# An attention and two mixture stages on one core: the first stage re-ordered, and one group's H spilled in two parts

## The chip, the cores and the metric

One core of a Trainium2 chip runs the whole program. The time is device microseconds of one execution, the median over several runs. TensorE (PE) multiplies matrices into PSUM; VectorE (DVE) and ScalarE (ACT) read PSUM; GpSimd (POOL) works on SBUF; SyncE (SP) issues most of the loads. Each engine takes its instructions in a fixed order.

## The reference, cut to what matters

Three stages follow each other; `x` of a stage is the output of the one before.

```python
    scale = 1.0 / np.sqrt(D)
    scores = scale * np.matmul(q, k.transpose(0, 1, 3, 2))
...
    keep = is_sink | in_window
    scores = np.where(keep, scores, -1000000000.0)
    scores = scores - np.max(scores, axis=-1, keepdims=True)
    a = np.exp(scores)
    a = a / (np.sum(a, axis=-1, keepdims=True) + 1e-09)
    return np.matmul(a, v).astype(np.float32)
...
    h = np.maximum(np.maximum(x @ w1, x @ w2), x @ w3)
    return (h @ w_out).astype(np.float32)
...
    for e in range(E):
        mask = assigned == e
        h = np.maximum(x[mask] @ w1[e], 0.0)
        out[mask] = h @ w2[e]
```

q, k and v are 4 x 8 x 768 x 64 (batch, heads, positions, head size), the window is 128, the sinks are 4. The rows of the attention are 3072 x 512; d_ff is 768 in the second stage; the third has 8 experts of at most 384 tokens, and each token goes to one.

## The kernel before, in words

Attention runs in 32 units. A unit is one batch, one half of 384 positions and one pair of heads: `load`, `prep`, `score`, `soft`, `pv`. Four units (p = 0 to 3) make a group g, which is a block of 384 tokens by 512; the 8 groups are called a0 to a7 in the order strings. The units of a0 and a1 are "native": their products are made in plain fp32, with no split of q and k (`native=8`). The later units split each operand into a rounded high part and the rest (h and l), and multiply three of the four products.

Moe1 takes a group's four x tiles, splits each into `xh`, `xl` (L265 to L269), and makes for each of six slices f three sums of 12 products (L280), whose maximum `m` (L282, L283) is one slice of H. H is split into h and l as well, and `x2` (L294) multiplies it with the out weights, 18 products for each of six sums (L305). The 18 weight slices come as words of 8 bytes, and `single` and `split` turn each into fp32 and then into h and l: one load (L220), DVE (L225, L227), ACT (L226, L212) and POOL (L228, L213). The first four loads land in a ring that later becomes the tile HL. The six out-weight slices (`load_out`) go through two buffers `st` of the pool conv, and start with transposes and small products that use a PSUM tile of the scores.

HL is not free while the ring is in use. So group 0 writes its six `m` slices to DRAM (L285), group 1 keeps its H in HL, and after group 1's x2 the six slices of group 0 are loaded (`reload`, L317), split by ACT (L323) and DVE (L324) into HL, and multiplied.

The order of the work is written as two strings, of units and of weight slices (`w` is one f of the three matrices, `o` one out-weight slice), and a planner inside the block (`schedule_with_timeline_sim`) lays the instructions out engine by engine from its own timeline. Some instructions are emitted with priority. SP's and ACT's transfers stand in the same orders as all else that the engine issues, so a transfer that has to wait for its buffer holds what stands behind it.

In `score` (L110) a block of scores that isn't the first of its half is copied from PSUM by ACT (L134), and then DVE writes the masked block over it (L135). T, the tile of probabilities, has three buffers for all units.

Of the kernel before, what the change touches and what calls it, by code (L numbers as in the profile page):

```python
# [22 lines left out]
def f32(ap): return ap.bitcast(FT)  # L23
def flip(nc,out,x,ident):
    nc.tensor.transpose(out,x,f32(ident))  # L25

class Attn:
    def __init__(s, tc, q,k,v,vs, keep, consts, pst, psp, pss, psv, work):
        s.tc=tc; s.nc=nc=tc.nc; s.q,s.k,s.v,s.vs=q,k,v,vs
        s.pst,s.psp,s.pss,s.psv,s.w=pst,psp,pss,psv,work  # L30
        jp=work.tile([128,128],I32,name="jp",tag="qs0",bufs=2)
        nc.gpsimd.iota(jp,pattern=[[1,128]],base=0,channel_multiplier=-1)
        s.ident=keep.tile([128,128],FR,name="ident")
        nc.vector.tensor_scalar(s.ident,jp,0.0,None,op0=OP.is_equal)
# [12 lines left out]
        s.kf=[]; s.kz=[s.zeros([consts.tile([128,4,132],FR,name=f"kz{h}") for h in range(2)])]  # L47
        t=consts.tile([1,1],FT,name="one"); nc.vector.memset(t,0.0)
        nc.scalar.activation(t,t,AF.Exp)
        s.n=0; s.no=('kh0','kh1')  # L50
        s.extra=None
# [8 lines left out]
    def load(s,b,hf,p,native=False):  # L60
        nc=s.nc; w=s.w
# [11 lines left out]
        else:  # L73
            u['kn']=w.tile([128,4,132],FT,name="kn",bufs=1)
            nc.sync.dma_start(u['kn'][:,:nb],s.k[i,:,:nb*132].rearrange("p (c j) -> p c j",j=132))
            u['qn']=w.tile([128,384],FT,name="qn",bufs=1)
            nc.sync.dma_start(u['qn'],s.q[i])
            u['vn']=w.tile([128,4,2,64],FT,name="vn",bufs=1)
# [31 lines left out]
    def score(s,u):  # L110
# [4 lines left out]
        for i in range(3):  # L115
# [4 lines left out]
            for h in range(2):  # L120
# [11 lines left out]
                else:  # L132

                    nc.scalar.activation(t[:,132*h:132*h+132],ps[:,128*h:128*h+132],AF.Copy)  # L134
                    nc.vector.copy_predicated(block,s.ca[:,h,:],ps[:,132-132*h:260-132*h])  # L135
# [12 lines left out]
    def pv(s,u,x):  # L148
# [9 lines left out]
        for h in range(2):  # L158
# [8 lines left out]
            if nat:  # L167
# [3 lines left out]
                for c,n,q,blk in jobs:  # L171
                    nc.tensor.matmul(po[a,q:q+n],u['vn'][:,blk,h,:],Af[:,c:c+n],start=False,stop=True,skip_group_check=True)  # L172
                if h==1: nc.scalar.activation(x,po[:,:384],AF.Copy)
                continue
# [7 lines left out]
            nc.tensor.matmul(po[:,:384],u['VK'][:,h,:],PB,start=False,stop=True,skip_group_check=True)  # L182
            nc.scalar.activation(x[a,:],po[o,:384],AF.Copy)
            nc.vector.tensor_tensor(x[a,:],po[a,:384],x[a,:],op=OP.add)

# [17 lines left out]
class Moe1:  # L203
    def __init__(s, tc, words,wgate, consts, wpool, main, conv, mm, pt, pss, ident):
        s.tc=tc; s.nc=tc.nc; s.mm=mm; s.pss=pss; s.main=main; s.conv=conv; s.ident=ident; s.consts=consts
        s.src=words; s.wgate=wgate
        s.W=[[wpool.tile([128,4,768],FR,name=f"w{i}{x}") for x in "hl"] for i in range(3)]
        s.WO=None; s.at=None; s.stage=None; s.HL=None; s.n=0
        s.WG=main.tile([128,6,16],FR,name="wgt")
# [4 lines left out]
    def single(s,src,ring=False):  # L214
# [4 lines left out]
        else: st=s.conv.tile([128,512,2],I32,name="st",bufs=2)  # L219
        nc.sync.dma_start(st.rearrange("p n t -> p (n t)"),src.bitcast(I32))  # L220
        A=s.pss.tile([128,512],FT,name="ps").bitcast(I32); C=st[:,:,0]
# [6 lines left out]
        nc.gpsimd.tensor_tensor(R,R,C,op=OP.add)  # L228
        return R.bitcast(FT)
    def part(s,x,f):  # L230
        return s.HL[:,"hl".index(x)*6+f]
# [28 lines left out]
    def group(s,xs,spill=None,pool=None,mid=None,between=None):  # L260
# [3 lines left out]
        for p in range(4):  # L264
            h=main.tile([128,384],FR,name=f"xh{p}",bufs=1); l=main.tile([128,384],FR,name=f"xl{p}",bufs=1)  # L265
            with s.tc.high_priority():
                nc.scalar.activation(h,xs[p],AF.Copy)  # L267
                nc.vector.tensor_tensor(l,xs[p],f32(h),op=OP.subtract)  # L268
            X.append((h,l))  # L269
        H=[]  # L270
        if s.HL is None and spill is None: s.HL=main.tile([128,12,384],FR,name="HL")
        for f in range(6):
            if between is not None: between(f)
            m=main.tile([128,384],FT,name="hm",bufs=2)
            for i in range(3):
# [8 lines left out]
                if mid is not None and (f,i)==s.at: mid()  # L284
            if s.HL is None: nc.scalar.dma_start(spill[f],m); continue  # L285
            h,l=(pool.tile([128,384],FR,name=f"h{x}{f}",bufs=1) if pool else s.part(x,f) for x in "hl")
            with s.tc.high_priority():
# [29 lines left out]
    def reload(s,spill):  # L317
        nc=s.nc; H=[]
# [304 lines left out]

def attention_mixtures(tc,q,k,v,vs,words,wg,u1,u2,out,off=60,spread=(0,1,3,4),native=8,order='a0 a0 a0 a0 w a1 w a1 w w a1 w w a1 a2',order1='a2 o o o o o o a2 a2',back=1,at=(1,0),s1=300,s2=400,nring=6):
    nc=tc.nc
    PS=bass.MemoryType.PSUM
    with ExitStack() as ctx:
# [12 lines left out]
        def att(g,p):  # L640
            xs.setdefault(g,[])
            u=A.load(g//2,g%2,p,4*g+p<native); A.prep(u); A.score(u); A.soft(u)
            x=main.tile([128,384],FT,name=f"x{p}")
            A.pv(u,x); xs[g].append(x)
        def lw(f): M.load_w(f)
        def lo(f): M.load_out(f)
        with tc.block(schedule_with_timeline_sim=True):
            A.extra=Spare(main)
            A.kf=[A.zeros([A.extra.tile([128,4,132],FT,tag=f'kf{i}{h}') for h in range(2)]) for i in range(3)]
            def emit(o,p):  # L650
                n=cnt[o]=cnt.get(o,-1)+1
# [11 lines left out]
            for o in order.split(): emit(o,False)  # L663
            rest=None
            for g in range(NG):
# [7 lines left out]
                d = g>=NG-3  # L673
                if g==0: sp=[dram.tile([128,384],FT,name=f"sp{f}") for f in range(6)]
                if g==NG-3: sp2=[[dram.tile([128,384],FT,name=f"sp{f}{x}") for x in "hl"] for f in range(6)]
                if g==NG-1:
# [3 lines left out]
                    r=Route(tc,LG,rt,rw,rc)  # L680
                H6,H=H if g==NG-1 else None,M.group(xs[g],sp if g==0 else sp2 if g==NG-3 else None,hp if g==NG-1 else None,rest,between)
                while late: between(spread[0])
# [39 lines left out]
        M.x2(H6,T7-3,LG,x2d,256,hp)  # L722
        M.by_rows(sp2,T7-6,x2d,acc,hp)
        with tc.high_priority(): fet(0)
# [64 lines left out]
```

## Time and profile before

| what | value |
|---|---|
| median of 3 runs | 983.9 us (982.41 to 985.26) |
| the profiled execution | 985.81 us, of which 984.0 us are the span from the first to the last instruction |
| PE busy | 937.8 us (95%), 6552 products |
| DVE, ACT, POOL busy | 687.8, 533.8, 348.8 us |
| mean granted TensorE clock | 0.977 of full speed |

PE is busy for nearly the whole span, so what counts is where it isn't, and where its clock is granted at half. Times below are from the start of the span. The prediction takes them from four kinds of views: busy time in stretches, waits by engine, groups of instructions by line, and instructions in order of time.

### The profile page before, as it was taken

The page shows a single profiled execution, that of the slowest core. Times are in us where ns is not written, and L with a number is a line of the kernel's source. Part 1 is how long each engine was busy: PE and PEld are TensorE (multiplying, and loading weights), DVE is VectorE, ACT ScalarE, POOL GpSimd, SP SyncE. Part 2 cuts the span into 40 slices and gives each one's busy share as a digit, 9 for nine tenths or more (in the row PEclk, how much of TensorE's full clock was granted, in tenths as well). Part 3 has the DMA queues.
Part 4 walks back from the last instruction along what each step waited for, and adds up shares of the span by engine and source line. Part 5 has one row for each costly group of instructions (what it writes and reads, how often), then busy time and mean ns, then how long its engine had stood idle before and what let it go on. Part 6 is the DMA issues. An engine that isn't in the chain of part 4 may idle for free.

```text
span 984.0 us, 18469 instructions
## 1 busy us (share of the span) xinstructions
PE 937.8 (95%) x6552; PEld 857.8 (87%) x6552; DVE 687.8 (70%) x1807; ACT 533.8 (54%) x1425; POOL 348.8 (35%) x317
## 2 busy tenths in 40 slices
PE   5889999969999999999999999999999999999996
PEld 4568989959999999999999998888888888888895
DVE  3897676687879976776764344879989889873320
ACT  4666664788789777677663211233433434344431
POOL 3578357145555535425434000011113032043331
PEclk8899999989999999999999999999999999999999
DMA  7455121222112112112110002544345352454420
GB/s 226 151 170 172 50 77 64 68 83 88 53 40 78 52 49 73 28 48 81 64 50 12 1 1 76 164 154 130 119 149 174 98 172 99 160 189 154 135 81 32
DMA packets 50541, 95.03 MB, mean 97 GB/s; under 512 B 6704, under 2 KB 20784, under 8 KB 50448
## 3 DMA queue, kind: packets, MB, share of 16 engines
q1 hardware_dynamic: 40560, 71.57, 23.4%
q0 software_dynamic: 3840, 12.45, 3.6%
q10 hardware_dynamic: 6048, 9.83, 2.7%
q8 instruction: 51, 0.84, 0.4%
q14 instruction: 42, 0.34, 0.1%
HBM read 77.84 MB, written 16.12 MB: 95 GB/s over the span
## 4 chain that ended last, share of the span: by engine, by line
PE 75%; DVE 8%; ACT 6%; issue 5%; DMA 4%; POOL 1%; SPq 1%; POOLq 0%; ACTq 0%; DVEq 0%
PE mm L280 28%; PE mm L608 11%; PE acc L601 11%; PE mm L305 7%; PE po L181 3%; PE rc L406 2%; PE pt L25 2%; PE pp L25 2%; PE po L172 2%; PE ps L126 1%; PE ps L127 1%; DMA sa<-in_u_dram 1%; PE ps L123 1%; DVE A_w L163 1%; DVE qs L97 1%
## 5 line engine op out<-in xcount | busy, mean ns | idle before, releaser
L601 PE MATMUL acc<-wbh,HL 128*128 128x512 f32 x384 | 131.1, 398 | 0.0
L177 POOL TENSOR_TENSOR L<-A_w,H 128x768 fp32r<-128x768 f32 x46 | 87.0, 1891 | 101.5 <-ACT H L176 91.1
L283 DVE TENSOR_TENSOR hm<-mm,hm 128x384 f32<-128x384 f32 x96 | 53.3, 555 | 68.6 <-PE mm L280 65.1
L620 POOL DMA_INDIRECT out_dram<-og,idx x24 | 32.2, 1340 | 180.6 <-ACT og L619 177.3
L305 PE MATMUL mm<-woh,HL 128*128 128x260 f32 (+1 forms) x432 | 89.5, 296 | 2.0 <-DVE HL L324 1.1
L552 ACT ACTIVATE wah<-sa 128x512 fp32r<-128x512 f32 x64 | 40.5, 632 | 89.6 <-PE mm L608 72.2
L601 PEld LDWEIGHTS acc<-wbh,HL 128*128 128x128 f32 x384 | 71.5, 188 | 12.8
L552 ACT ACTIVATE wbh<-sb 128x512 fp32r<-128x512 f32 x64 | 40.4, 631 | 74.9 <-PE acc L601 72.0
L601 PE MATMUL acc<-wbl,HL 128*128 128x512 f32 x192 | 76.9, 401 | 0.0
L305 PEld LDWEIGHTS mm<-woh,HL 128*128 128x128 f32 x432 | 72.3, 198 | 3.3 <-DVE HL L324 1.4
L608 PE MATMUL mm<-HL,wah 128*128 128x384 f32 x256 | 68.5, 343 | 0.0
L280 PE MATMUL mm<-xh,w0h 128*128 128x384 f32 x192 | 66.8, 348 | 1.2 <-ACT xh L267 0.6
L280 PE MATMUL mm<-xh,w1h 128*128 128x384 f32 x192 | 66.7, 347 | 0.8 <-ACT hm L282 0.5
L280 PE MATMUL mm<-xl,w0h 128*128 128x384 f32 x192 | 65.5, 341 | 1.9 <-DVE xl L268 1.9
L280 PE MATMUL mm<-xh,w2h 128*128 128x384 f32 x192 | 67.0, 349 | 0.0
L280 PE MATMUL mm<-xh,w1l 128*128 128x384 f32 x192 | 65.5, 341 | 0.0
L280 PE MATMUL mm<-xl,w2h 128*128 128x384 f32 x192 | 65.5, 341 | 0.0
L553 DVE TENSOR_TENSOR wbl<-sb,wbh 128x512 fp32r<-128x512 f32 x64 | 43.9, 688 | 30.7 <-ACT wbh L552 30.7
L280 PE MATMUL mm<-xl,w1h 128*128 128x384 f32 x192 | 65.1, 339 | 0.0
L280 PE MATMUL mm<-xh,w0l 128*128 128x384 f32 x192 | 65.1, 339 | 0.0
L280 PE MATMUL mm<-xh,w2l 128*128 128x384 f32 x192 | 65.1, 339 | 0.0
L612 DVE SCALAR_TENSOR_TENSOR HL<-mm,HL 128x384 fp32r<-128x384 f32 x64 | 35.5, 554 | 40.8 <-ACT HL L611 40.6
(320 smaller groups left out, 2888.3 us busy)
## 6 DMA issues: line engine op xcount, KB each, us to landing
sa<-in_u_dram SPq DMA_DIRECT2D x64, 256.0 KB
sb<-in_u_dram SPq DMA_DIRECT2D x64, 256.0 KB
HL<-in_words_dram SPq DMA_DIRECT2D x18, 512.0 KB
qn<-in_q_dram SPq DMA_DIRECT2D x24, 192.0 KB
x2d<-xo ACTq DMA_DIRECT2D x15, 256.0 KB
kn<-in_k_dram SPq DMA_DIRECT2D x12, 264.0 KB
st<-in_words_dram SPq DMA_DIRECT2D x6, 512.0 KB
vn<-in_v_dram SPq DMA_DIRECT2D x12, 256.0 KB
```

The costliest lines, as they stand in the source:

```text
L25: nc.tensor.transpose(out,x,f32(ident))
L177: nc.gpsimd.tensor_tensor(L,Af,f32(H),op=OP.subtract)
L181: nc.tensor.matmul(po[:,q:q+n],u['VS'][:,blk,128*h:128*h+128],part[:,c:c+n],start=(part is H and j==0),stop=False,skip_group_check=True)
L280: nc.tensor.matmul(ps[:,:384],s.W[i][a][:,p,f*128:(f+1)*128],X[p][b],start=(n==0),stop=(n==11)); n+=1
L283: else: nc.vector.tensor_tensor(m,ps[:,:384],m,op=OP.max)
L305: nc.tensor.matmul(ps[:,:n],H[f][a][:,t*128:(t+1)*128],s.WO[b][:,f,u,c],start=(k==0),stop=(k==17)); k+=1
L552: nc.scalar.activation(h,src,AF.Copy)
L553: (nc.gpsimd if s.n>=6 and nm=="wa" else nc.vector).tensor_tensor(l,src,f32(h),op=OP.subtract)
L601: s.mms.append(nc.tensor.matmul(acc[t],H[f][a][:,t*128:(t+1)*128],W[f][1][b],start=(f==0 and n==0),stop=(f==F-1 and n==2))); n+=1
L608: s.mms.append(nc.tensor.matmul(ps[:,:384],W[f][0][a][:,k,:],X[k][b],start=(n==0),stop=(n==11))); n+=1
L612: nc.vector.scalar_tensor_tensor(l,ps[:,:384],0.0,f32(h),op0=OP.max,op1=OP.subtract)
L620: st=nc.gpsimd.indirect_dma_start(out=s.out,out_offset=bass.IndirectOffsetOnAxis(ap=idx[:,t:t+1],axis=0),in_=o,in_offset=None)
```

## The change

Six edits, all in the attention and moe1 block.

1. The score copies of the first four units go from ACT to DVE.
2. The units of a1 move ahead by one or two places among the weight slices.
3. `pv` of a0's units writes the pair `xh`, `xl` straight from PSUM (`split`: ACT copies, DVE subtracts), so `group` has nothing left to split there.
4. Two orders of loads are given to the planner: the first a2 unit's k and q loads come after the last word load of the ring, and an out-weight load after the sixth word load from the end. The two memsets of `kz` come after the six of `kf`.
5. Group 0's H is split at once into `hp` tiles, which take the `st` buffers of conv, and both parts are written to DRAM: 12 transfers of 192 KB in place of 6.
6. `reload` only loads, 12 transfers: f 0 to 3 into the `xh`, `xl` tiles, f 4 and 5 into HL. ACT and DVE have nothing to do there.

```diff
+def split(nc,hl,x):
+    nc.scalar.activation(hl[0],x,AF.Copy)
+    nc.vector.tensor_tensor(hl[1],x,f32(hl[0]),op=OP.subtract)
...
-            nc.sync.dma_start(u['kn'][:,:nb],s.k[i,:,:nb*132].rearrange("p (c j) -> p c j",j=132))
+            ld=[nc.sync.dma_start(u['kn'][:,:nb],s.k[i,:,:nb*132].rearrange("p (c j) -> p c j",j=132))]
-            nc.sync.dma_start(u['qn'],s.q[i])
+            ld.append(nc.sync.dma_start(u['qn'],s.q[i]))
+            if s.behind is not None:
+                for x in ld: s.tc.add_manual_dep(x.ins,s.behind.ins.name,mybir.DependencyInfo(mybir.DependencyClass.NoSync,mybir.DependencyReason.DATA),reason="order of loads")
+                s.behind=None
...
-                    nc.scalar.activation(t[:,132*h:132*h+132],ps[:,128*h:128*h+132],AF.Copy)
+                    if u['n']<4: nc.vector.tensor_copy(t[:,132*h:132*h+132],ps[:,128*h:128*h+132])
+                    else: nc.scalar.activation(t[:,132*h:132*h+132],ps[:,128*h:128*h+132],AF.Copy)
...
-                if h==1: nc.scalar.activation(x,po[:,:384],AF.Copy)
+                if h==1:
+                    for c in x: split(nc,c,po[:,:384]) if type(c) is tuple else nc.scalar.activation(c,po[:,:384],AF.Copy)
...
-        nc.sync.dma_start(st.rearrange("p n t -> p (n t)"),src.bitcast(I32))
+        ld=nc.sync.dma_start(st.rearrange("p n t -> p (n t)"),src.bitcast(I32))
+        if ring: s.loads.append(ld)
+        else: s.tc.add_manual_dep(ld.ins,s.loads[-6].ins.name,mybir.DependencyInfo(mybir.DependencyClass.NoSync,mybir.DependencyReason.DATA),reason="order of loads")
...
-            if s.HL is None: nc.scalar.dma_start(spill[f],m); continue
-            h,l=(pool.tile([128,384],FR,name=f"h{x}{f}",bufs=1) if pool else s.part(x,f) for x in "hl")
+            if s.HL is None: h,l=(s.conv.tile([128,2,384],FR,name="hp",tag="st",bufs=2)[:,x] for x in range(2))
+            else: h,l=(pool.tile([128,384],FR,name=f"h{x}{f}",bufs=1) if pool else s.part(x,f) for x in "hl")
...
-            m=s.main.tile([128,384],FT,name="hm",bufs=2)
-            nc.sync.dma_start(m,spill[f])
-            h,l=s.part("h",f),s.part("l",f)
-            nc.scalar.activation(h,m,AF.Copy)
-            nc.vector.tensor_tensor(l,m,f32(h),op=OP.subtract)
-            H.append((h,l))
+            H.append([s.main.tile([128,384],FR,name=f"x{x}{f}",bufs=1) if f<4 else s.part(x,f) for x in "hl"])
+            for d,x in zip(spill[f],H[f]): s.nc.sync.dma_start(f32(x),d)
...
+            A.zeros(A.kz[0])
...
+                if o=='a2': A.behind=M.loads[-1]
...
+                if g in (0,NG-3): sp=[[dram.tile([128,384],FT,name=f"sp{g}{f}{x}") for x in "hl"] for f in range(6)]
...
-order='a0 a0 a0 a0 w a1 w a1 w w a1 w w a1 a2'
+order='a0 a0 a0 a0 w a1 w a1 w a1 w a1 w w a2'
```

## Rows read from the trace of the kernel before

**Rows 1.** Busy time in stretches, whole span; after the bounds PE, PEld, DVE, ACT, POOL.
```profile
0.00:36.00 36.00, 23.83 (x77) 16.12 (x77) 19.27 (x60) 20.85 (x75) 13.97 (x27) 0.76 0.64 194
36.00:68.00 32.00, 26.33 (x124) 18.15 (x125) 28.09 (x50) 21.08 (x74) 23.15 (x23) 0.95 0.57 182
68.00:124.00 56.00, 56.00 (x324) 50.06 (x323) 41.81 (x84) 35.08 (x108) 36.35 (x36) 1.00 0.34 112
124.00:181.00 57.00, 55.26 (x357) 53.17 (x356) 37.94 (x78) 32.83 (x78) 32.06 (x29) 1.00 0.21 66
181.00:237.00 56.00, 47.77 (x339) 45.16 (x339) 45.40 (x86) 50.18 (x156) 21.39 (x16) 0.88 0.28 86
237.00:320.00 83.00, 81.74 (x568) 80.69 (x568) 68.35 (x132) 70.21 (x206) 44.61 (x40) 1.00 0.19 58
```

**Rows 2.** What PE waited for, 0 to 36 us; total, times, longest.
```profile
PE ps L123 <- POOL woh L53: 4.8, 1, 4.8
PE ps L123 <- DVE T_w L135: 1.7, 1, 1.7
PE ps L123 <- DVE wol L135: 1.3, 1, 1.3
PE ps L123 <- DMA qf<-in_q_dram: 0.5, 1, 0.5
```

**Rows 3.** Groups of ACT, 0 to 36 us; the idle time before them stands last.
```profile
L134 ACT ACTIVATE T_w<-ps 128x132 f32<-128x132 f32 x12 | 3.1, 270 | 6.9 <-PE ps L123 6.8
L226 ACT ACTIVATE HL<-HL 128x512 int32<-128x512 uint32 x4 | 2.6, 660 | 5.0 <-DMA HL<-in_words_dram 5.0
L94 ACT ACTIVATE kh_w<-kn 64x396 fp32r<-64x396 f32 x4 | 2.1, 529 | 0.1
```

**Rows 4.** Groups of DVE, 0 to 36 us.
```profile
L135 DVE COPY_PREDICATED T_w<-ca,ps 128x128 f32<-128x128 uint8 x10 | 2.9, 301 | 4.4 <-ACT T_w L134 4.3
```

**Rows 5.** SP's transfers in order of time: start, time taken to issue.
```profile
14.93 0.35 SPq L71 DMA_DIRECT2D qf<-in_q_dram  x1
15.85 0.58 SPq L75 DMA_DIRECT2D kn<-in_k_dram  x1
64.08 12.31 SPq L220 DMA_DIRECT2D HL<-in_words_dram  x5
```

**Rows 6.** Short stretches: PE's busy time and, third from the end, its clock.
```profile
12.00:16.00 4.00, 1.60 (x7) 0.97 (x7) 0.99 (x5) 3.02 (x15) 0.00 (x0) 1.00 0.95 284
20.00:32.00 12.00, 8.64 (x26) 5.65 (x28) 7.53 (x20) 11.22 (x44) 1.84 (x3) 0.50 0.65 189
208.00:212.00 4.00, 3.30 (x16) 3.30 (x17) 4.00 (x7) 3.11 (x15) 2.35 (x2) 0.53 0.33 90
220.00:224.00 4.00, 2.87 (x13) 2.87 (x14) 3.84 (x8) 3.21 (x11) 3.48 (x3) 0.50 0.40 104
```

**Rows 7.** What PE waited for, 36 to 68 us.
```profile
PE mm L280 <- DVE xl L268: 1.9, 3, 1.1
PE mm L280 <- ACT xh L267: 0.6, 1, 0.6
```

**Rows 8.** POOL and ACT in order of time: the last weight slice, the sixth slice's eviction.
```profile
102.31 1.28 POOL L213 TENSOR_TENSOR w2l<-HL,w2h 128x512 fp32r<-128x512 f32 x1
117.24 0.49 ACT L282 ACTIVATE hm<-mm 128x384 f32<-128x384 f32 x1
```

**Rows 9.** Groups of ACT, 181 to 237 us.
```profile
L323 ACT ACTIVATE HL<-hm 128x384 fp32r<-128x384 f32 x6 | 3.1, 516 | 2.1 <-DMA hm<-sp 2.1
L94 ACT ACTIVATE kh_w<-kn 64x528 fp32r<-64x528 f32 x8 | 5.1, 641 | 0.1
```

**Rows 10.** What PE waited for, 181 to 237 us.
```profile
PE ps L126 <- DVE T_w L135: 4.3, 3, 2.0
PE mm L305 <- DVE HL L324: 1.1, 1, 1.1
```

**Rows 11.** A group of the page's costliest, whole span.
```profile
L283 DVE TENSOR_TENSOR hm<-mm,hm 128x384 f32<-128x384 f32 x96 | 53.3, 555 | 68.6 <-PE mm L280 65.1
```

More of the change, by code (lines that the diff above doesn't have):

```diff
@@ L46, in __init__ @@
             t=consts.tile([128,384],FR,name=f"psb{i}"); nc.vector.memset(f32(t),0.0); s.pb.append(t)
-        s.kf=[]; s.kz=[s.zeros([consts.tile([128,4,132],FR,name=f"kz{h}") for h in range(2)])]
+        s.kf=[]; s.kz=[[consts.tile([128,4,132],FR,name=f"kz{h}") for h in range(2)]]
         t=consts.tile([1,1],FT,name="one"); nc.vector.memset(t,0.0)
         nc.scalar.activation(t,t,AF.Exp)
-        s.n=0; s.no=('kh0','kh1')
+        s.behind=None; s.n=0; s.no=('kh0','kh1')
         s.extra=None
@@ L182, in pv @@
             nc.tensor.matmul(po[:,:384],u['VK'][:,h,:],PB,start=False,stop=True,skip_group_check=True)
-            nc.scalar.activation(x[a,:],po[o,:384],AF.Copy)
-            nc.vector.tensor_tensor(x[a,:],po[a,:384],x[a,:],op=OP.add)
+            nc.scalar.activation(x[0][a,:],po[o,:384],AF.Copy)
+            nc.vector.tensor_tensor(x[0][a,:],po[a,:384],x[0][a,:],op=OP.add)
 class Spare:
@@ L207, in __init__ @@
         s.W=[[wpool.tile([128,4,768],FR,name=f"w{i}{x}") for x in "hl"] for i in range(3)]
-        s.WO=None; s.at=None; s.stage=None; s.HL=None; s.n=0
+        s.WO=None; s.at=None; s.stage=None; s.HL=None; s.n=0; s.loads=[]
         s.WG=main.tile([128,6,16],FR,name="wgt")
@@ L229, in single, with pair @@
         return R.bitcast(FT)
+    def pair(s,p):
+        return tuple(s.main.tile([128,384],FR,name=f"x{x}{p}",bufs=1) for x in "hl")
     def part(s,x,f):
@@ L264, in group @@
         for p in range(4):
[L265 to L269, printed above, removed]
+            if type(xs[p]) is tuple: X.append(xs[p]); continue
+            X.append(s.pair(p))
+            with s.tc.high_priority(): split(nc,X[p],xs[p])
         H=[]
@@ L317, in reload @@
     def reload(s,spill):
-        nc=s.nc; H=[]
+        H=[]
         for f in range(6):
-            m=s.main.tile([128,384],FT,name="hm",bufs=2)
-            nc.sync.dma_start(m,spill[f])
-            h,l=s.part("h",f),s.part("l",f)
-            nc.scalar.activation(h,m,AF.Copy)
-            nc.vector.tensor_tensor(l,m,f32(h),op=OP.subtract)
-            H.append((h,l))
+            H.append([s.main.tile([128,384],FR,name=f"x{x}{f}",bufs=1) if f<4 else s.part(x,f) for x in "hl"])
+            for d,x in zip(spill[f],H[f]): s.nc.sync.dma_start(f32(x),d)
         return H
@@ L622, in expert, with attention_mixtures @@
             s.scat.append(st)
-def attention_mixtures(tc,q,k,v,vs,words,wg,u1,u2,out,off=60,spread=(0,1,3,4),native=8,order='a0 a0 a0 a0 w a1 w a1 w w a1 w w a1 a2',order1='a2 o o o o o o a2 a2',back=1,at=(1,0),s1=300,s2=400,nring=6):
+def attention_mixtures(tc,q,k,v,vs,words,wg,u1,u2,out,off=60,spread=(0,1,3,4),native=8,order='a0 a0 a0 a0 w a1 w a1 w a1 w a1 w w a2',order1='a2 o o o o o o a2 a2',back=1,at=(1,0),s1=300,s2=400,nring=6):
     nc=tc.nc
@@ L642, in att @@
             u=A.load(g//2,g%2,p,4*g+p<native); A.prep(u); A.score(u); A.soft(u)
-            x=main.tile([128,384],FT,name=f"x{p}")
-            A.pv(u,x); xs[g].append(x)
+            x=main.tile([128,384],FT,name=f"x{p}") if g else M.pair(p)
+            A.pv(u,[x]); xs[g].append(x)
         def lw(f): M.load_w(f)
@@ L662, in emit @@
                         A.kz.append(A.zeros([A.extra.tile([128,4,132],FR,name=f'kz{h}b') for h in range(2)]))
-            for o in order.split(): emit(o,False)
+            for o in order.split():
+                if o=='a2': A.behind=M.loads[-1]
+                emit(o,False)
             rest=None
@@ L673, in attention_mixtures @@
                 d = g>=NG-3
-                if g==0: sp=[dram.tile([128,384],FT,name=f"sp{f}") for f in range(6)]
-                if g==NG-3: sp2=[[dram.tile([128,384],FT,name=f"sp{f}{x}") for x in "hl"] for f in range(6)]
+                if g in (0,NG-3): sp=[[dram.tile([128,384],FT,name=f"sp{g}{f}{x}") for x in "hl"] for f in range(6)]
                 if g==NG-1:
@@ L680, in attention_mixtures @@
                     r=Route(tc,LG,rt,rw,rc)
-                H6,H=H if g==NG-1 else None,M.group(xs[g],sp if g==0 else sp2 if g==NG-3 else None,hp if g==NG-1 else None,rest,between)
+                H6,H=H if g==NG-1 else None,M.group(xs[g],sp if g in (0,NG-3) else None,hp if g==NG-1 else None,rest,between)
                 while late: between(spread[0])
@@ L722, in attention_mixtures @@
         M.x2(H6,T7-3,LG,x2d,256,hp)
-        M.by_rows(sp2,T7-6,x2d,acc,hp)
+        M.by_rows(sp,T7-6,x2d,acc,hp)
         with tc.high_priority(): fet(0)
```

## The prediction

> **What bounds the kernel now.** I read the busy time by stretch first [rows 1]. PE is busy for 937.8 of 984.0 us, so the change can only win what PE doesn't use, and the stretches say where that is. From 0 to 36 us PE is busy 23.83 of 36, at a clock of 0.76. From 36 to 68 it stands idle for 5.7 us. From 68 to 181 it is full but for 1.7. From 181 to 237 it idles 8.2 at a clock of 0.88, and there ACT is the busiest engine, 50.18 of 56. From 237 to 320 it idles 1.3, and the code behind 237 us is hardly touched. So the whole sum is made in two places, the first 68 us and 181 to 237.
>
> Then I read the waits and groups of those places. In the first 36 us PE waits for masked score blocks [rows 2]; DVE, which writes them, waits 4.3 us for ACT's copies [rows 4]; and ACT, in its fixed order, stood 5.0 us in front of word conversions whose transfers hadn't landed [rows 3]. That is a stall on loads that nobody needed yet, handed from ACT to DVE to PE. [...]
>
> **First 36 us: copies to DVE, order of loads.** Sixteen copies leave ACT (0.27 us each, 4.3 in all [rows 3]). On DVE I price each like its masked copy of nearly the same size out of PSUM, 0.30 us [rows 4]: 4.8 us. DVE is busy 19.27 of 36 there [rows 1], so they lie in idle time; without that cover the cost would be the 4.8. What goes for certain is PE's wait on blocks that came late through ACT, 1.7 + 1.3, and on q, 0.5 [rows 2]: the q load issued at 14.93 has k of an a2 unit right behind it [rows 5], which the change sends away. Low end 3.5 us. High end: the work that PE did in 36 us, at full clock. A mean of 0.76 between the levels 1 and 0.5 is 48% of 36 us at half clock, 17.3 us. Of these, 20 to 32 hold 8.64 busy us, which would be 4.3 shorter; the other 5.3 us, as busy as those, 1.9. So 23.83 - 6.2 = 17.6 us of work after a start at 4.8 could end at 22.4, which is 13.6 earlier. I take 7.5: the 3.5 and four of the 6.2 that the clock costs. I don't take more, because the fourth unit's scores need one of three T buffers, which the first unit frees only after its softmax and its transposes, and that chain stays. It is what's late next. Weight conversion begins behind the fourth unit's scores, so it moves along.
>
> The `kz` memsets now stand behind those of `kf`. PE's first wait of 4.8 us is put down to POOL [rows 2]. The gain lies between nothing (its first q may land no earlier) and two memsets, 1.1 us. I take 0.
>
> **Pairs straight from PSUM.** PE waited 1.9 + 0.6 us for the split of group 0's x [rows 7]. One ACT pass of 0.5 us goes from each of the four chains; the subtraction stays. Between 0 and 2.5; I take 1.5, since the last of the four is the one on which the stage's end hangs.
>
> **What moves to later.** The first a2 unit's k and q are now loaded behind the last ring load, so its four k copies (2.1 us of ACT [rows 3]) and their like leave the first 36 us. They fall in 68 to 181 us, where ACT is idle for 45 of 113 [rows 1]: 0. Uncovered they would cost about 3. The a1 units move ahead of weight slices. The last slice is ready at 103.6; the sixth f is evicted at 117.2, its twelve products having begun some 2 us before [rows 8]. That is 11.5 us of room, so 0.
>
> **Spill in two parts.** Six ACT copies (0.52 [rows 9]), six subtractions (0.56 [rows 11]) and six more issues (0.35 [rows 5]) go to 68 to 124 us, where ACT idles 21 us and DVE 14 [rows 1]. The cost lies between nothing and 6 x 1.08 = 6.5, if each delays an eviction on which a PSUM buffer hangs. I take 0.5. The `hp` tiles hold the out weights' buffers until they have been written, so the first two out-weight loads come later than they did; both were early, and I take 0.
>
> **Reload.** ACT loses 3.1 us of copies and 2.1 of waiting [rows 9], and DVE six subtractions. PE's own wait for the last of them is 1.1 us, but its larger waits (4.3) are for score blocks that come through the same ACT [rows 10]. Low end 1.1. High end: the 8.2 idle, and half of what ran at the low clock (3.30 and 2.87 us at 0.53 and 0.50 [rows 6], 3.0): 11.2. As ACT sets the pace, I take what ACT gets back, 5.0.
>
> Two waits are new. Group 2's splits can't begin before group 0's x2 has read `xh`, `xl`, and behind them stand group 2's first products. The first pair costs 0.52 + 0.56 us, all four 4 x 0.52 + 0.56 = 2.6 if nothing hides them; x2's products after its last use of the first tile hide some. Between 0 and 2.6; I take 1.0. And f 4 and 5 can be loaded only when group 1's x2 has read HL. ACT's two waits on such loads made 2.1 us [rows 9]; x2 now has four other slices to begin with. Between 0 and 2.1; I take 1.0. On SP these loads stand in front of k and q loads of later units.
>
> **Sum.** -7.5 - 1.5 + 0.5 - 5.0 + 1.0 + 1.0 = -11.5 us. The profiled execution took 985.81 (span 984.0); it would take 974.3. It lay 1.9 above the median of 983.9, so for a median I say 972.5. A difference within 0.3%, 3 us, can't be told from none.
>
> **Rivals.** *The stall changes its place (0.20).* The T buffers and the first unit's softmax set the first stage, and DVE, now with copy, mask and maximum, is late in ACT's stead. For it: most of PE's waits there are already on DVE [rows 2]. Against it: DVE idles 16.7 of 36 [rows 1]. Then the first stage gives 3.5 and the pairs nothing: -3.5 + 0.5 - 5.0 + 2.0 = -6.0, 978.
>
> *The weights become the bound (0.08).* If conversion keeps its old times, PE can come forward by its 11.5 us of room [rows 8] and no more, and a1 units ahead of slices take up half of that: -5.8 + 0.5 - 5.0 + 2.0 = -8.3, 975.5. Against it: conversion hangs on the same scores as PE.
>
> *All of it goes (0.10).* First stage 11, pairs 2.5, reload 8, costs 1: -20.5, 963.5.
>
> *Slower (0.14): SP stands still.* Word loads wait on SP for their place in the ring, up to 12.31 us in one row [rows 5], and what stands behind them waits too. Where PE comes earlier and POOL's conversion does not, such holds grow, and the q and v loads of a1 units sit behind them. For it: the holds are there now. Against it: PE is full from 68 to 124 in spite of them [rows 1]. If PE waits out one hold of that size and another half as long, it loses 18.5: -11.5 + 18.5 = +7.0, 991. It decides from 11.5 us of such waiting on.
> [...]
>
> **How the numbers follow.** My forecast has 0.48, with its own range of 966 to 979 (first stage 4 to 10, reload 2 to 8). The range leaves out most of the slower case and part of the largest gain: 961 to 985. Forecast, the first two rivals and the largest gain are faster, less 0.08 for gain and cost that cancel: faster 0.78, same 0.08, slower 0.14.
>
> **What would show it.** Right: from 0 to 36 us PE at a clock near 1 and no wait that goes back to ACT behind words; the first weight conversion on DVE well ahead of its old place behind the fourth unit's scores; the sixth slice's first eviction some 9 us before 117.2; from the end of group 1's products to group 2's first less than 56 us, at a clock above 0.95, with no wait on score blocks of 2 us. Wrong: low clock again in the first 30 us, PE waiting for xh or xl at group 2's start for more than 2 us, or PE waiting on q or v loads in the first 120.

## The result, and the profile after

The changed kernel takes 995.95 us (median of 5 runs, 992.07 to 998.14), the kernel before 984.71 beside it: ratio 1.0107, 95% interval 1.0086 to 1.0129. It is slower by 11 us, where 11.5 us less were forecast. The profiled execution took 994.76 us, with a span of 993.0 at a mean clock of 0.982; 9.0 us of span are to be found.

The busy time in stretches, the view of [rows 1], of the changed kernel; after the bounds PE, PEld, DVE, ACT, POOL, then the granted clock:

```profile
0.00:36.00 36.00, 24.61 (x107) 16.71 (x107) 25.85 (x82) 14.83 (x55) 15.25 (x30) 0.91 0.59 167
36.00:68.00 32.00, 29.29 (x152) 22.51 (x150) 26.21 (x52) 23.88 (x81) 26.30 (x25) 1.00 0.62 200
68.00:124.00 56.00, 51.23 (x289) 45.43 (x288) 45.16 (x78) 34.09 (x101) 32.77 (x33) 0.97 0.38 119
124.00:181.00 57.00, 54.45 (x353) 53.79 (x352) 36.93 (x79) 33.35 (x82) 31.33 (x27) 0.97 0.33 103
181.00:237.00 56.00, 48.57 (x351) 45.13 (x350) 39.88 (x81) 49.34 (x154) 19.09 (x15) 0.97 0.31 95
237.00:320.00 83.00, 79.25 (x536) 77.65 (x537) 68.71 (x120) 63.15 (x186) 42.73 (x39) 0.98 0.19 55
320.00:557.00 237.00, 229.06 (x1507) 223.95 (x1506) 168.49 (x324) 158.29 (x455) 99.78 (x84) 0.99 0.16 48
```

Against [rows 1] the reader sees three things. The start is better: 107 products in the first 36 us where 77 stood, at 0.91 for 0.76. From 68 to 124 us PE, which had been full, idles 4.8 us. And behind 237 us, where the prediction looked for nothing, PE idles 3.8 us to 320 and 7.9 more to 557; in the kernel before it was 1.3 and 2.5.

What PE waited for in the changed kernel, in 68 to 124, 124 to 181, 181 to 237, 237 to 320 and 440 to 480 us (total, times, longest):

```profile
PE mm L291 <- DVE wol L138: 3.0, 1, 3.0
PE ps L133 <- DVE qs L104: 1.6, 1, 1.6
...
PE mm L291 <- ACT hm L293: 2.6, 1, 2.6
...
PE po L190 <- DVE x L193: 1.7, 1, 1.7
PE ps L133 <- DVE T_x L143: 1.0, 1, 1.0
...
PE mm L316 <- DVE hm L294: 2.8, 1, 2.8
...
PE ps L133 <- DVE T_w L143: 3.8, 2, 3.7
```

In place of the 4.3 us for score blocks that led [rows 10] stand a 1.0 and other small ones; single waits of about 3 us stand in stretches that had none.

Stretches can't say how far ahead a kernel is, so I use a yardstick. Every product in PE's records counts by its columns, 2400 of them as one us; that is a scale of mine and not a rate measured (in the kernel before, at a clock of 1.00, a product of L280 with 384 columns takes 175 ns, the median from one start to the next). Transposes and the products of the native units count twice (by the same median 256 columns take 216 ns there in L172 and 120 in L181, 128 columns 109 in a transpose and 60 in L181). The sum is the same in every kernel here. The table has the time at which a given part of that sum was done: absolute for the kernel before, and for the others the difference to it. Mark 70 lies in group 0's products, 90 just behind them, 150 at the end of group 1's x2, between 150 and 170 lies the reloaded group's x2, 230 is in group 2's x2, and 490 at the end of group 7's sums. Each line is one profiled execution, and the ratio, against the kernel before on the same chip, is from all of a kernel's runs. Six of the lines, the two with hp_own, kz_only, before_off, fa_off92 and after_off88, are from chips on which the kernel before takes 992 to 993 us; as far as before_off tells, whose order is nearly that of the kernel before, they lose it behind mark 490 (it is 0.6 us ahead there, and its span is 9.7 us longer). So the columns up to 490 can be compared.

```
mark of PE's work (us)   70     90    150    170    230    250    490   ratio measured
before                 105.6  127.6  201.0  236.5  306.1  328.3  598.4
changed kernel         -11.4   -3.6   -1.0  -10.7   -0.3   -1.0   +7.3  1.0107
a2_early                -8.9   -8.5   -4.0  -15.7   -0.6   -1.1   +0.2  1.0003
first_only             -11.4   -2.3   +1.2   -2.2   +0.4   -0.1   +2.1  0.9997
first_only_a2_early    -10.9  -10.6  -11.6  -12.7  -12.2  -11.8   -3.5  1.0004
spill_only              -2.9   -2.5   +9.3   +0.5   +7.6   +7.1   +8.3  1.0101
spill_only_hp_own       +0.3   +0.3   +4.4   -7.9   +3.8   +3.2  +14.5  1.0130
a2_early_hp_own         -6.4   -6.2   -0.1  -11.7   -2.4   -3.0   +7.2  1.0091
kz_only                 +0.3   +0.3   +0.3   -1.0   -0.5   -0.2   +7.8  1.0086
before_off              -1.0   -1.0   -1.0   -0.7   -0.6   -0.6   -0.6  1.0008
fa_off92                -9.3   -9.0   -9.8  -10.9   -4.9   -4.8   -5.2  0.9983
after_off88            -10.2   +0.4   +2.9   -6.1   +3.8   +5.8   +9.9  1.0069
kz_pin                  -4.5   -4.5   -4.5   +3.2   +5.1   +5.1   +5.6  1.0084
after_pin              -11.3   -1.9   -1.8  +13.6  +15.4  +15.4  +15.9  1.0150
fa_pin                  -8.1   -7.8   -8.7   -0.9   +0.9   +1.0   +0.8  1.0002
before_apin             -1.4   -1.4   -1.6   -1.8   +8.7   +8.1  +16.9  1.0180
fa_pin3                 -9.0   -8.7   -9.6  -10.7   -8.7   +3.1   +3.5  1.0050
after_pin3             -11.1   -2.4   +0.2   -9.2   +1.6  +13.6  +14.0  1.0116
before_apin3            -0.1   -0.1   -0.1   -0.7   -0.3   +5.9  +13.9  1.0174
ae_pin3                 -5.9   -5.6   +0.2  -11.4   -5.9   +2.0   +2.4  1.0017
```

The changed kernel's line is the case in short. It was 11.4 us ahead. It lost 7.8 between marks 70 and 90, gained 9.7 between 150 and 170 (the reload) and gave that back by 230, and then, level with the kernel before, lost 7.6 in groups 3 to 7, whose code the diff doesn't touch. The 1.7 us that the span is longer still came in the expert stage and were not followed up.

The first loss in the changed kernel's instructions in order of time, on DVE, POOL and SP, and then what SP and ACT waited for:

```profile
95.22 7.26 DVE L102 TENSOR_TENSOR kz<-kn,kh_w 64x396 fp32r<-64x396 f32 x2
102.51 1.14 DVE L104 TENSOR_TENSOR qs<-qn,qs 64x384 fp32r<-64x384 f32 x2
...
94.79 1.29 POOL L222 TENSOR_TENSOR w2l<-HL,w2h 128x512 fp32r<-128x512 f32 x1
96.04 0.46 POOL L109 TENSOR_TENSOR vk<-vns,vk 40x128 fp32r<-40x128 f32 x1
96.45 1.51 POOL L155 TENSOR_TENSOR T_w<-T_w,l 128x792 f32<-128x792 f32 x1
97.92 1.31 POOL L239 TENSOR_TENSOR cA<-cA,HL 128x512 int32<-128x512 int32 x1
99.19 1.29 POOL L222 TENSOR_TENSOR w0l<-cA,w0h 128x512 fp32r<-128x512 f32 x1
100.44 1.01 POOL L116 TENSOR_TENSOR vsp<-vn,vsp 128x384 fp32r<-128x384 f32 x1
...
89.11 0.43 SPq L81 DMA_DIRECT2D qn<-in_q_dram  x1
...
103.67 0.33 SPq L81 DMA_DIRECT2D qn<-in_q_dram  x1
...
SPq L79 <- DVE kz L102: 9.4, 1, 9.4
...
ACT qs L103 <- DMA qn<-in_q_dram: 8.5, 1, 8.5
```

The moved loads are issued at 88.64 and 89.11 us ([rows 5] have the first of them at 15.85). Their two subtractions take 7.26 us together, under six POOL instructions without a gap, and end a microsecond after the last of them; `qs` comes some 6 us late, and PE waits 1.6 for it. The unit behind uses the same single buffers `kn` and `qn`. SP stands 9.4 us at its k load, until the second subtraction has read `kn`, and the q behind it is issued only at 103.67. ACT, in its fixed order, stands 8.5 us in front of that q; DVE's masked block and the weight slice that ACT converts next both come late behind it, and PE waits the 3.0 of the first row.

### The profile page after: what moved, and what is told of

Same layout as the page of the kernel before. It is cut to its first block, busy times and chain, and to the rows that moved or that the text cites. A ratio compares the mean times of both kernels' runs of the same rounds, so it can differ in the third digit from the quotient of the medians.

```text
span 993.0 us, 18476 instructions
## 1 busy us (share of the span) xinstructions
PE 935.6 (94%) x6552; PEld 856.3 (86%) x6552; DVE 700.3 (71%) x1823; ACT 528.4 (53%) x1405; POOL 348.7 (35%) x317
## 4 chain that ended last, share of the span: by engine, by line
PE 65%; ACT 10%; DVE 10%; issue 7%; DMA 5%; POOL 1%; SPq 1%; ACTq 0%; POOLq 0%; DVEq 0%
PE mm L291 22%; PE mm L615 11%; PE acc L608 11%; PE mm L316 5%; PE rc L413 2%; PE po L190 2%; PE pt L25 2%; PE po L180 1%; PE ps L130 1%; DMA sa<-in_u_dram 1%; ACT T_x L152 1%; DMA qf<-in_q_dram 1%; DVE qs L104 1%; PE pp L25 1%; ACT T_w L152 1%
## 5 line engine op out<-in xcount | busy, mean ns | idle before, releaser
L316 PE MATMUL mm<-woh,HL 128*128 128x260 f32 (+1 forms) x384 | 79.9, 296 | 4.5 <-DVE hm L294 2.8
L316 PEld LDWEIGHTS mm<-woh,HL 128*128 128x128 f32 x384 | 64.1, 196 | 5.9 <-DVE hm L294 3.0
```

What stands on the lines that cost most here:

```text
L316: nc.tensor.matmul(ps[:,:n],H[f][a][:,t*128:(t+1)*128],s.WO[b][:,f,u,c],start=(k==0),stop=(k==17)); k+=1
```

## The experiments

Each ratio is against the kernel before on the same chip. Theories: A, the moved a2 loads; B, later D, the order that the planner lays anew; C, the spill's buffers and the reload; R, the later stretch can't use a lead whatever its order.

**Parts of the change.** `a2_early`:

```diff
-                if o=='a2': A.behind=M.loads[-1]
```

> The changed kernel (995.9 us), but the first a2 unit's k and q are loaded as soon as SP comes to them, as before; all else stays changed. Theory A (the moved loads: k and q issued at 88.64 and 89.11 us put that unit's subtractions into the time in which POOL converts words, where two of them took 7.26 us each for 0.55, and hold back the next unit's q): the 7.8 us lost between 94 and 124 us come back, some 988; group 0's last product near 115 instead of 123.2. Theory B (the order written for the later groups is what costs, +8 us behind 306 us, whatever the edits): the stretch to 124 us may get better, and the end stays near 994 to 997. Theory C (spill in two parts and out weights late): no change at 124 us, 996.

Measured: 985.43 us, ratio 1.0003 (0.9982 to 1.0024). (The text above has 7.26 us for each of the two subtractions; it is both together.) The two are back in the start, and take half a microsecond each; the line's instructions in this kernel:

```profile
23.23 0.52 DVE L102 TENSOR_TENSOR kz<-kn,kh_w 64x396 fp32r<-64x396 f32 x1
26.29 0.58 DVE L102 TENSOR_TENSOR kz<-kn,kh_w 64x396 fp32r<-64x396 f32 x1
```

At mark 90 the lead is 8.5 in place of 3.6, so A holds for its place. But at mark 230 both kernels are level with the kernel before, and the whole 10 us of difference in the totals came behind that: 0.8 us against 7.6 lost up to mark 490, and the rest in the expert stage. The total confirmed A's number (988) and the table says that it did so for another reason.

`first_only` has the old spill and the old reload in the changed kernel, `first_only_a2_early` the early a2 loads as well; `spill_only` is the kernel before with edits 5 and 6 alone.

> The changed kernel with the old spill (one tensor, no hp tiles) and the old reload (six loads into hm, ACT copies, DVE subtractions): the first stage, its order, the pairs and the moved loads alone. Theory A (moved loads): the loss between 94 and 124 us stays, the reload's 9.7 us at 226 us never come, the end is near 996 or a little above. Theory C (the spill's hp tiles and the reload into xh and xl make groups 0 and 2 wait): group 0 ends some 6 us earlier, and the end is near 985. Theory B (order of the later groups): anything from 985 to 998, with the difference made behind 306 us.

> The changed kernel with the old spill and reload and with the first a2 unit's k and q loaded early: the copies on DVE, the kz memsets behind those of kf, the new order of a1 units and weight slices, the pairs, and the out weights' loads behind the words. Theory A: the first stage's 11 us last to 124 us and beyond, 974 to 979. Theory B: the 11 us are there at 124 us and gone at the end, 983 or more. Theory C agrees with A here: 974 to 979.

> The kernel before with the spill in two parts and the reload by transfers alone, nothing else. Theory A: the reload's gain is there at 226 us (9.7) and part of it stays, since the a2 units are not late: 978 to 982. Theory C: slower than before, 988 to 992. Theory B (order of the later groups): the gain at 256 us is 3 or more, and the end is near or above 984 all the same, lost behind 306 us.

Measured: 984.92 us, 0.9997 (0.9969 to 1.0025); 984.64 us, 1.0004 (0.9981 to 1.0027); 994.54 us, 1.0101 (1.0058 to 1.0145). The pair first_only and first_only_a2_early shows A: 2.3 ahead at mark 90 against 10.6, with nothing in the text of the two but those loads between them. The planner's order differs as well, but the stumble is the same one: in first_only one of the subtractions takes 6.59 us and ACT stands 8.7 us in front of the next q; in first_only_a2_early both subtractions stay under 0.6. The totals alone would have told otherwise: first_only has the number of C. And first_only_a2_early keeps 12 us to mark 230, and loses 8.7 behind it, so that its total has the number of B. spill_only loses 11.8 us between marks 90 and 150, which is C. Two of SP's transfers in it, in order of time:

```profile
125.58 1.47 SPq L220 DMA_DIRECT2D st<-in_words_dram  x2
...
137.01 0.33 SPq L220 DMA_DIRECT2D st<-in_words_dram  x1
```

The first two out-weight loads, at 21.98 and 23.60 in the kernel before, wait for `hp` to give the `st` buffers back. PE waits from 124 to 140 us for POOL, DVE, ACT and POOL (2.1, 1.7, 1.2, 1.0, the last for the conversion of such a word), and ACT then stands 2.7 us in front of the next. In the changed kernel no more than 2.6 us are lost between marks 90 and 150.

**The suspects taken away, and two controls.** In `spill_only_hp_own` and `a2_early_hp_own` the spill uses no `st` buffer:

```diff
-            if s.HL is None: h,l=(s.conv.tile([128,2,384],FR,name="hp",tag="st",bufs=2)[:,x] for x in range(2))
+            if s.HL is None: h,l=s.main.tile([128,520],FT,name="xo",bufs=1)[:,:384].bitcast(FR),m.bitcast(FR)
```

`kz_only` is the kernel before with the two `kz` memsets behind those of `kf` and nothing else; `before_off` is the kernel before with `off=64` for `off=60`, a number of the planner's alone.

> The kernel before with the spill in two parts and the reload by transfers alone, but the two parts are no longer written into buffers of the out weights' loads: H goes into the xo buffer (idle in group 0) and L in place into hm. Theory C (the hp tiles keep the out weights' loads back, 125.58 us instead of 22 to 24, and their conversions then crowd ACT and DVE at the start of group 1, where PE loses 13 us): those 13 us are not lost, and of the reload's gain something stays: 980 to 984. Theory D (whatever is edited, the order of all instructions is laid anew, and where it leaves PE without other work at the end of a group, a wait of 2 to 4 us on DVE and a stretch at half clock follow): 985 to 995, with the first loads early and a loss all the same.

> The changed kernel with both suspects gone: the first a2 unit's k and q early, and the two parts of the spill in xo and hm. Theory A with C: 11 us ahead at 124 us and still at 181, the reload's gain on top, 970 to 976. Theory D: 10 or more ahead at 181 us, and given back in one to three stumbles between 230 and 480 us, at the ends of groups; 980 to 988.

> The kernel before with one edit that moves two POOL memsets (0.55 us each) behind six others, and nothing else. By every theory on the edits' own costs: 983 to 986, no difference. Theory D: the order behind it is laid anew, so it may move by 3 us or more to either side, with stumbles at other places than before.

> The kernel before with one number of the planner's changed (the head start in priority of the units' instructions, 60 to 64): the same instructions, data and buffers. By every theory on the edits' own costs: 983 to 986. Theory D: the time moves by 3 us or more, to either side, and the difference lies in waits of PE on DVE or ACT of 1 to 4 us with half clock behind them.

Measured: 1005.52 us, 1.0130 (1.0103 to 1.0156); 1001.14 us, 1.0091 (1.0062 to 1.0119); 1001.58 us, 1.0086 (1.0058 to 1.0114); 993.06 us, 1.0008 (0.9990 to 1.0026), beside 992.02 for the kernel before on this chip. C is half right: in the kernel before with the new spill, freeing the buffers leaves 4.1 us in place of 11.8 to go between marks 90 and 150. In the changed kernel with the early loads it wins nothing there (6.1 in place of 4.5). And both totals lie above every number that was expected. The kernel with both suspects gone, a2_early_hp_own, isn't faster: it loses 9.6 us behind mark 230. And two memsets of half a microsecond cost 8.3 us behind mark 230 in a kernel that until then is within 1.0 of the kernel before at every mark: D. `before_off` tells less than meant, since its order hardly changed (52 of PE's 2431 instructions from group 2 on stand elsewhere).

The planner's orders can be compared in the built programs. From group 3 on (3026 instructions of PE, DVE, ACT and POOL) kz_only and first_only_a2_early stand in the same order exactly, though one reaches mark 230 11.7 us before the other. So here is a pair that nobody arranged: one order, two arrival times. Their largest stumble, kz_only first: what PE waited for, then DVE and POOL in order of time, then 5 us of the stretch:

```profile
PE mm L305 <- DVE HL L289: 2.6, 1, 2.6
...
367.12 2.20 DVE L97 TENSOR_TENSOR qs<-qn,qs 64x384 fp32r<-64x384 f32 x1
...
367.04 1.86 POOL L177 TENSOR_TENSOR L<-A_w,H 128x768 fp32r<-128x768 f32 x1 [3.44 <-ACT H L176]
...
371.00:376.00 5.00, 3.28 (x17) 3.12 (x17) 4.43 (x11) 4.82 (x21) 0.28 (x1) 0.77 0.02 8
```

first_only_a2_early, the same views:

```profile
PE mm L316 <- DVE HL L300: 2.6, 1, 2.6
...
355.48 2.20 DVE L104 TENSOR_TENSOR qs<-qn,qs 64x384 fp32r<-64x384 f32 x1
...
355.40 1.87 POOL L186 TENSOR_TENSOR L<-A_w,H 128x768 fp32r<-128x768 f32 x1 [3.44 <-ACT H L185]
...
360.00:365.00 5.00, 3.91 (x19) 3.75 (x20) 4.28 (x11) 4.75 (x19) 0.45 (x2) 0.69 0.02 6
```

Same place, same wait, same lengths, 11.6 us apart: a DVE subtraction of 0.55 us takes 2.20 under a POOL instruction of 1.86, all behind it on DVE is late, PE waits 2.6 for the last slice of H, and the clock in the five us shown is 0.77 and 0.69. Between marks 230 and 490 one loses 8.3 and the other 8.7. R falls with this pair: the lead of 11.7 us is still 11.3 at mark 490.

**Orders pinned.** These kernels take the order of another one on PE, DVE, ACT and POOL, by such an edge between each two neighbours:

```diff
+            tc.add_manual_dep(t[b],t[a].name,mybir.DependencyInfo(mybir.DependencyClass.NoSync,mybir.DependencyReason.DATA),reason="order of another kernel")
```

From group 2 on: `kz_pin`, `after_pin` and `fa_pin` are kz_only, the changed kernel and first_only_a2_early in the order of the kernel before; `before_apin` is the kernel before in the changed kernel's order.

> The kernel before with its two kz memsets moved (as in kz_only, ratio 1.0086), but on PE, DVE, ACT and POOL the instructions that groups 2 to 7 issue (2431, 540, 651 and 130) stand in the order of the kernel before. If the order laid anew costs (theory D): ratio 0.998 to 1.002. If the moved memsets themselves cost, by something that I don't see: 1.006 to 1.011.

> The changed kernel, complete, with the order of the kernel before on PE, DVE, ACT and POOL for what groups 2 to 7 issue. Theory D (the later groups' order costs, not the edits): ratio 0.990 to 1.002, without the 4 us lost near 442 to 470 us. Theory R (the reload's lead can't be kept, because the attention units on ACT and DVE set the pace to 306 us, and the spill crowds group 1's start): equal to the kernel before at 306 us, and no gain on it, 1.000 to 1.011, depending on what the order adds.

> The changed kernel with the old spill and reload and the a2 loads early (as in first_only_a2_early, 1.0004), with the order of the kernel before for groups 2 to 7. Theory D: its lead of 12 us at 306 us is kept to the end, ratio 0.986 to 0.991. Theory R: the lead goes between 306 and 480 us in waits of PE on DVE and ACT, since the units are no earlier than before: 0.996 to 1.002.

> The kernel before, none of the edits, with the changed kernel's order on PE, DVE, ACT and POOL for what groups 2 to 7 issue. Theory D: slower by what the changed kernel loses behind 306 us, 1.005 to 1.009. If the later loss belongs to the edits: 0.998 to 1.002.

Measured: 1.0084 (1.0053 to 1.0116), 1.0150 (1.0104 to 1.0196), 1.0002 (0.9983 to 1.0020), 1.0180 (1.0141 to 1.0220). The totals speak against D or for neither: kz_pin has the number of the other theory, fa_pin that of R, after_pin none, and before_apin is slower as D has it, but by twice as much. The table says where these numbers come from. From mark 230 to 490 the three with the order of before lose 0.5, 0.5 and -0.1 us, though they arrive 14.5 us apart, and before_apin loses 8.2 (the changed kernel: 7.6). But between marks 150 and 170, where pinned and free instructions meet, the three lose 7.7, 15.4 and 7.8. The same from group 3 on, to move that seam:

> The changed kernel with the old spill and reload and the a2 loads early (as first_only_a2_early), with the order of the kernel before on PE, DVE, ACT and POOL for what groups 3 to 7 issue. first_only_a2_early was 12 us ahead at 306 us and lost 9 of them to the end. Theory D (the order laid anew for the later groups lost them): the 12 us last, 972 to 976, ratio 0.986 to 0.991. Theory R (the later stretch can't use a lead, whatever its order): 0.997 to 1.002.

> The changed kernel, complete, with the order of the kernel before for what groups 3 to 7 issue. It stood 0.3 us ahead at 306 us and lost 7.6 behind that. Theory D: no loss behind 306 us, ratio 0.997 to 1.003. Theory R: as the changed kernel, 1.008 to 1.012.

> The kernel before, none of the edits, with the changed kernel's order for what groups 3 to 7 issue. Theory D: it loses what the changed kernel loses behind 306 us, 6 to 8 us, ratio 1.006 to 1.009. Theory R: 0.998 to 1.002.

> The changed kernel with the a2 loads early (as a2_early), with the order of the kernel before for what groups 3 to 7 issue. It differs from fa_pin3 by the spill in two parts and the reload by transfers alone. a2_early stood 0.6 us ahead at 306 us. If spill and reload cost the 11.6 us by which it is behind first_only_a2_early there: 983 to 985, ratio 0.998 to 1.001. If that difference, too, is only an order: 973 to 980.

Measured: 1.0050 (1.0023 to 1.0076), 1.0116 (1.0079 to 1.0152), 1.0174 (1.0125 to 1.0224), 1.0017 (0.9998 to 1.0037). The seam came along, and costs 6.2 to 12.0 us between marks 230 and 250; so no total with a pinned order says what an edit is worth. As totals, fa_pin3 and before_apin3 have the number of neither theory, after_pin3 has that of R, and ae_pin3 lies just above the slower of its two cases. Behind the seam, from 250 to 490, the three in the order of before lose 0.4 each. before_apin3, which has none of the edits, loses 8.0, and the changed kernel in its own order 8.3. Its largest stumble, DVE and POOL of the changed kernel in order of time:

```profile
443.20 0.56 DVE L300 TENSOR_TENSOR HL<-hm,HL 128x384 fp32r<-128x384 f32 x1
443.79 3.83 DVE L102 TENSOR_TENSOR kz1b<-kn,kh_x 64x528 fp32r<-64x528 f32 x1
...
443.21 0.69 POOL L108 CAST vk<-vns 40x128 fp32r<-40x128 f32 x1 [4.41 <-PE po L191]
443.88 1.81 POOL L186 TENSOR_TENSOR L<-A_w,H 128x768 fp32r<-128x768 f32 x1
445.64 0.46 POOL L109 TENSOR_TENSOR vk<-vns,vk 40x128 fp32r<-40x128 f32 x1
446.05 1.00 POOL L116 TENSOR_TENSOR vsp<-vn,vsp 128x384 fp32r<-128x384 f32 x1
```

And of before_apin3, the wait of PE first:

```profile
PE ps L126 <- DVE T_w L135: 3.7, 1, 3.7
...
450.07 3.84 DVE L95 TENSOR_TENSOR kz1b<-kn,kh_x 64x528 fp32r<-64x528 f32 x1
...
450.16 1.82 POOL L177 TENSOR_TENSOR L<-A_w,H 128x768 fp32r<-128x768 f32 x1
451.95 0.44 POOL L102 TENSOR_TENSOR vk<-vns,vk 40x128 fp32r<-40x128 f32 x1
452.36 0.98 POOL L109 TENSOR_TENSOR vsp<-vn,vsp 128x384 fp32r<-128x384 f32 x1
```

It is the 3.7 us wait of the changed kernel, carried by the order into a kernel without the change. At this one place the changed kernel loses 5.8 of its 7.6 us and before_apin3 6.8 of its 8.0 (on the yardstick, between 438 and 450 us of the kernel before).

**Other orders, planned whole.** `fa_off92` is first_only_a2_early with `off=92`, `after_off88` the changed kernel with `off=88`.

> The changed kernel with the old spill and reload and the a2 loads early (first_only_a2_early), planned with a head start of 92 for the units in place of 60: the planner lays the later groups out in another order, 508 of some 3000 neighbouring pairs away from that of before where first_only_a2_early is 837 away. Theory D: the lead at 306 us (12 us) is kept as far as this order loses less than first_only_a2_early's 8.7 us: 973 to 981, ratio 0.988 to 0.996. Theory R: the lead goes all the same, 0.998 to 1.003.

> The changed kernel, complete, planned with a head start of 88 in place of 60, which lays the later groups nearly in the order of before (307 pairs away; the changed kernel's own order is 812 away). Theory D: the 7.6 us behind 306 us aren't lost, ratio 0.996 to 1.003. Theory R: 1.008 to 1.012, as the changed kernel.

Measured, 5 rounds: 992.14 us beside 993.09, ratio 0.9983 (0.9967 to 0.9999); 1000.59 us, 1.0069 (1.0042 to 1.0097). By its total fa_off92 has the number of R. The table has it otherwise: it loses nothing behind mark 230, as D has it, but gives up 4.9 of 9.8 us between 150 and 230 already; it is the fastest kernel of the study, by less than 0.3%. after_off88 is a miss for D as I put it: an order near that of before by neighbours loses 6.1 us all the same, so nearness doesn't tell a good order.

## Why the prediction was wrong, step by step

**What bounds the kernel.** The step that failed most is the sentence "the code behind 237 us is hardly touched. So the whole sum is made in two places". The code is untouched; its order isn't, because the planner lays out the whole block. That cost the changed kernel 7.6 us (mark 230 to 490), shown by before_apin3 and by kz_only. No term of the sum and no rival had it.

**First 36 us, and pairs.** Right in direction: -9.0 for both together, 11.4 measured at mark 70. No run had the copies or the pairs alone, and spill_only and kz_pin, which have neither, stand 2.9 and 4.5 us ahead at mark 70, so a part of the 11.4 may be the order's. The clock of the first 36 us is 0.91. The first weight conversion on DVE comes 3.2 us earlier, not "well ahead", and ACT now stands 11.5 us in front of words, but PE no longer waits behind it: the stall in the profile grew while what hung on it went. The sixth slice's first eviction stood at 117.24 [rows 8] and is at 112.20, 5 us earlier where 9 were foretold; the loss to the moved loads lies between.

**"What moves to later ... 0"** failed, by 7.8 us (8.3 in the pair). The step named ACT's idle time as the cover [rows 1]. The moved work that mattered was DVE's, on operands that stand in SBUF, and there POOL, which I didn't look at, was busy without a gap (from 94.79 to 101.45 us, while two subtractions took 7.26 together). And it priced the moved copies, not who shares the loads' buffers: the next unit's k and q.

**Spill.** +0.5, "the first two out-weight loads come later ... both were early, and I take 0". Alone, it cost 11.8 us (spill_only), of which 7.7 are gone when the `st` buffers are left free. In the changed kernel at most 2.6 show, and why so few was not tried; a2_early, whose group 0 isn't held, loses 4.5. The high end of that term, 6.5, held the wrong thing, ACT's and DVE's passes instead of the loads that hp holds back. What the remaining 4.1 are wasn't told apart.

**Reload.** -5.0, and +2.0 for the two new waits. The signs set for it all came: 41 us from group 1's products to group 2's first (177.3 to 218.1) where 56 stood, a clock of 1.00 in them, no wait on score blocks above 1.0. Between marks 150 and 170 the six kernels with the new reload that the planner ordered whole gain 8.8 to 12.3 us (after_pin, whose seam lies there, loses). By mark 230 those six have given back 7.1 to 15.1, and the sum over both is between -2.3 and +3.4. The kernels with the old reload that were planned whole gain at most 3.4 there. Group 2's splits in the changed kernel (ACT in order of time), and busy time with PE first and its clock:

```profile
217.50 1.35 ACT L28 ACTIVATE xh<-x 128x384 fp32r<-128x384 f32 x3
...
232.37 0.51 ACT L28 ACTIVATE xh<-x 128x384 fp32r<-128x384 f32 x1
...
208.00:216.00 8.00, 8.00 (x69) 8.00 (x68) 4.06 (x8) 6.61 (x16) 4.07 (x3) 1.00 0.09 34
216.00:224.00 8.00, 6.80 (x44) 5.91 (x42) 6.27 (x9) 6.11 (x16) 4.92 (x4) 1.00 0.29 85
224.00:232.00 8.00, 4.39 (x26) 3.28 (x26) 6.85 (x12) 6.17 (x21) 4.62 (x5) 1.00 0.25 70
232.00:240.00 8.00, 7.24 (x35) 6.77 (x36) 6.32 (x15) 7.85 (x30) 3.38 (x3) 0.79 0.17 52
```

x2 of the reloaded group now ends at 219 us instead of 236, but the fourth x of group 2 is split only at 232.37, and between them PE has 4.39 us of work in 8, and in the next 8 us the clock is 0.79. The old reload had been what PE did while ACT and DVE finished the units. So the term was right at the place where it was read, ACT's time; what failed is that it was booked as the end's. That the units' order and not the reload sets this part is likely, as first_only_a2_early has its fourth split at 220.7 with the old reload, but it wasn't tried by itself.

**Rivals.** The slower one had the sign, and a place near to the first loss (ACT stood 8.5 us for a q load), and half the mechanism: SP did stand still with the q behind it, but at the next unit's k load, whose buffer the stretched subtraction held, and not at a word load. The 18.5 us of waiting that it named did not occur. (The 12.31 us of [rows 5] that it was scaled by are five loads in one row; the longest wait among them is 5.0 us.) "The stall changes its place" described a DVE that is late in the first stage; PE waits 2.1 us there for DVE's masked blocks, and it cost little.

**Sum of what was measured**, in steps of the table: -11.4 at mark 70, +7.8 moved loads, +2.6 to mark 150 (spill and what follows), -9.7 + 10.4 reload, +7.6 order, +1.7 behind mark 490: +9.0, the difference of the spans.

## What to carry to other kernels

Where a planner orders one block, an edit anywhere can change the order everywhere, and that can be worth more than the edit: two memsets cost 8.3 us here. So follow the lead along equal amounts of work, not the total alone, and look for a kernel with the same order before crediting or blaming an edit for a difference far from it. And price moved work by what runs beside it, not only by the idle time of its engine: ask what POOL does at the new time (here two subtractions took 7.26 us beside six POOL instructions, and half a microsecond each in a2_early), and who shares the moved load's buffer.

## What the runs showed of the hardware

In these traces a DVE subtraction with both operands in SBUF that started while a POOL instruction ran was often stretched, and the longest ended only after a run of POOL instructions had: in the changed kernel 3.83 us for `kz1b` where `kz0b`, of the same shape, had taken 0.69 two microseconds before, through three POOL instructions in a row, and 7.26 for two of 0.55 through six (6.66 and 0.57). The record has such an instruction's start and end, not what held it. I took each DVE instruction's time above the fastest fifth of its line and shape, where that is over 0.15 us, up to 600 us: 41.9 us in the kernel before and 52.9 in the changed one, and beside each of them POOL was busy for at least as long as the excess. Between 306 and 480 us it is 16.2 in the kernel before, 22.4 in the changed one, 24.5 in kz_only, but 21.7 in a2_early, which lost 0.8 us between marks 230 and 490; it depends on which instruction is hit. That these collisions are what makes an order bad is read from the rows of the two largest stumbles; no run took POOL's work away to show it.

Of the changed kernel's 170 subtractions with both operands in SBUF up to 600 us, the 106 without POOL's work beside them (memsets aside) and the 11 that started before a POOL instruction took at most 0.01 us above the fastest fifth; of the 53 that started while one ran, 40 took over 0.15 more, up to 6.11. The rows at 443 us have both cases. The subtraction at 443.20 was first and took 0.56, and the POOL cast at 443.21 took 0.69 where one like it had taken 0.29 (at 93.28). That cast was then running when `kz1b` started at 443.79, and `kz1b` ended at 447.62, 0.57 us behind the last of the three POOL instructions that followed the cast without a gap (443.88, 445.64 and 446.05).

Also unexpected: in these runs one order took the same time from three different starts. The three kernels pinned from group 3 to the order of before lose 0.4 us each from mark 250 to 490, some 270 us, though they arrive up to 11.6 us apart.
